# Attention windows as 64-row, 32- and 64-column products instead of zero-padded 128-row ones

## The chip, the core and the metric

The kernel runs on one core of a Trainium2 chip. The metric is the device time of one launch in microseconds. TensorE (PE in the profile) multiplies; VectorE (DVE), ScalarE (ACT) and GpSimd (POOL) do the elementwise work; SyncE (SP) issues nearly all DMAs. A matmul has a stationary operand, loaded into the array first (a weight load, PEld in the profile), and a moving operand that streams through; its result goes to one of eight PSUM banks of 128 partitions x 512 floats.

## What is computed

The reference, cut to what matters: attention in chunks of 32 queries over a window of 64 keys (8 memory keys, 16 to the left, the 32 of the chunk, 8 to the right), and then two feed-forward layers on 3072 tokens of 512 features.

```python
for c in range(nc):                       # 24 chunks of 32, for 4 batches and 8 heads of 64
    k_full = concat(mem_k, k[max(0, 32*c - 16) : min(S, 32*c + 40)])
    scores = matmul(q_c, k_full.T) / sqrt(D)
    a = softmax(scores)
    out[c] = matmul(a, v_full)
x = relu(out @ w_in)**2 @ w_out           # 512 -> 2048 -> 512
y = (silu(x @ w_gate) * (x @ w_val)) @ moe2_w_out   # 512 -> 1536 -> 512
```

Attention is in plain float32 on TensorE, where every matmul runs as two passes, each with its own weight load. The two layers split each operand into a high and a low part of the type float32r and sum three products.

## The kernel before

**Units.** Attention is cut into 24 units: 128 tokens (4 chunks) of one batch, all 8 heads. The host lays out, for each unit, `q`, `k` and `v` as 128 x 1024 floats. A partition of `q` and `k` is (one of two heads `hh`, one of 64 features); a partition of `v` is (one of two halves `m` of the heads, one of 64 keys of the window). Thus each 128-row operand holds two heads over each other.

**Scores** (`scores`, matmul at L544). For each of 16 (pair of heads, chunk) the stationary operand is 128 rows x 64 columns of `q`, the moving one 128 rows x 64 keys. So that the two heads stay apart, the host puts `q` down as a block diagonal: the 64 columns are 32 queries of the one head and 32 of the other, and half of the rows of each are zeros. The output stands in 64 PSUM partitions, alternately the lower and the upper half, so the array is used as two column halves of 128 rows x 64 columns.

**Weights** (`weigh`, L573 to L605). Maximum, subtract, Exp, sum, reciprocal, multiply, on a 128 x 512 tile `pt`, mostly on DVE.

**Turning.** The weights must stand with keys on partitions. Units 0 to 7 do that on TensorE (`turn_pe`, L644), and two copies of 64 x 512 (L653 on DVE, L655 on ACT) bring the result into a block-diagonal tile `pbd` (named `a` in the profile); the others use 16 transposes of 32 x 128 on DVE (`turn`, L622), which write into `pbd` as well. POOL sets two such tiles to zero at the start (L511), and only their blocks are ever written.

**Weighted sums** (`mixing`, matmul at L673). 16 matmuls: stationary 128 rows x 64 columns of `v`, moving 128 rows x 64 columns of `pbd`, again in two column halves, all into one PSUM bank.

**Leaving** (`leave`, L467 on ACT and L474 on DVE). The bank goes as a high and a low part, in one instruction of 512 columns on each engine, to the input tile `x` of the first layer. The last eight units go to DRAM by way of a copy (`leave_far`).

**The layers.** For four blocks of 512 tokens the first layer runs in the direct way: per hidden row block 12 matmuls of 512 columns into a hidden bank (L852), its ReLU, square and split on ACT, DVE and POOL, and 12 matmuls into four accumulating banks (L879), which lags two row blocks behind. In the first block the weights are decoded as they come (`prep1`, L731 to L819, which ends in the low part at L815). Then follow, from about 431 us, the rest of the first and all of the second layer with seven products in place of eight (L1108, L1245).

**What sets the order.** The code records operations with the engines that may do them and an estimated cost (`Plan.op`); a planner (`Plan.run`) then lays all of them out in one order for all engines, gives out the buffers, and keeps PE as busy as its costs say. `todo` says beside which hidden row block each step of a unit stands. From the second unit of the list `TURNS` on, the weighted sums of one unit and the scores of the next are one PE operation, with a planned cost of 2.2 us (L550), so that they stand directly behind each other; this is so 15 times. Buffers: twelve tiles `S0` for the `q`, `k`, `v` of the first four units, four tiles `A4` for the two `pbd` and the inputs of the rest, eight PSUM banks, of which the layer holds four for its accumulators.

The names in the rows: `ps` is a PSUM bank, `s` and `a` are tiles of `S0` and `A4`, `xx` and `x` the layer's inputs, `rp0` and so on decoded weights, `t` and `f` scratch tiles, `m` small statistics, `r` the split hidden values.

## Time and profile before

| what | value |
|---|---|
| time, median of 3 runs | 1105.41 us (1105.08 to 1106.93) |
| the profiled execution's own time | 1106.09 us |
| its span, first to last instruction | 1104.3 us |
| mean granted TensorE clock | 0.996 |
| PE busy | 1082.3 us, 98% of the span |
| PE weight loads busy | 892.0 us, 81% |
| DVE busy | 860.0 us, 78% |
| ACT busy | 594.1 us, 54% |
| DMA | 309.42 MB, mean 280 GB/s |

The shares are means over the whole program. A stage's own limit is read from the busy time by stretch, from the chain of work that ended last, and from who waits for whom. A group "x32" of L544 or L673 is 16 matmuls of two passes. Ends of matmuls are modelled in the profile, starts are not; lengths of groups are therefore best taken from start to start.

### The profile page before, as it was taken

The numbers are of one execution on the slowest core, as the hardware profiler recorded it, in microseconds if no ns is written. First come the engines' busy times: TensorE is split into PE (matmuls) and PEld (weight loads), VectorE is DVE, ScalarE is ACT, GpSimd is POOL, SyncE is SP. The second block draws the span as 40 slices with busy tenths as digits, with TensorE's granted clock in tenths as the row PEclk, the third lists the DMA queues.
The fourth block names the chain that finished last, engine by engine and source line by source line (L and its number), as shares of the span: only waits on it lengthen the run. The fifth ranks groups of instructions, "written<-read, shape, count | busy, mean of one in ns | idle before, by whom it ended". The sixth has DMA issues, their size and how long they took to land.

```text
span 1104.3 us, 17051 instructions
## 1 busy us (share of the span) xinstructions
PE 1082.3 (98%) x6044; PEld 892.0 (81%) x6044; DVE 860.0 (78%) x1540; ACT 594.1 (54%) x1010; POOL 126.5 (11%) x106
## 2 busy tenths in 40 slices
PE   5899999999999999999999999999999999999998
PEld 4778888888888888888888888888888887888886
DVE  6999878878879999778997667998769854534981
ACT  4888554554556566556654344564566633333650
POOL 2113101112011222001300000102310000000000
PEclk9899999999999999999999999999999999999999
DMA  9953487888889889999868999996998578655552
GB/s 362 409 222 113 134 278 242 296 294 300 306 277 344 288 285 342 393 344 348 290 225 266 404 406 395 328 357 224 358 335 298 161 241 307 213 195 172 190 169 99
DMA packets 133669, 309.42 MB, mean 280 GB/s; under 512 B 13136, under 2 KB 50000, under 8 KB 133584
## 3 DMA queue, kind: packets, MB, share of 16 engines
q1 hardware_dynamic: 133584, 308.33, 78.9%
q8 instruction: 48, 0.79, 0.3%
q14 instruction: 37, 0.30, 0.1%
HBM read 227.02 MB, written 81.26 MB: 279 GB/s over the span
## 4 chain that ended last, share of the span: by engine, by line
PE 95%; DMA 2%; ACT 1%; DVE 1%; issue 0%; SPq 0%; ACTq 0%
PE ps L1108 37%; PE ps L1245 22%; PE ps L852 16%; PE ps L879 15%; PE ps L673 2%; PE ps L544 2%; DMA rp0float<-in_w 1%; DMA s<-in_q 1%; ACT f L765 0%; SPq L525 0%; DVE u L486 0%; PE ps L644 0%; ACT f L772 0%; DVE f L486 0%; DVE rp3float32r L815 0%
## 5 line engine op out<-in xcount | busy, mean ns | idle before, releaser
L495 ACT ACTIVATE t<-ps 128x512 f32<-128x512 f32 x170 | 100.9, 596 | 218.4 <-PE ps L852 102.3
L486 DVE TENSOR_TENSOR t<-t,ps 128x512 f32<-128x512 f32 x72 | 49.1, 686 | 42.0 <-PE ps L1108 38.1
L622 DVE STREAM_TRANSPOSE a<-t 32x128 f32<-32x128 f32 x256 | 77.4, 303 | 4.3
L495 ACT ACTIVATE t<-t 128x512 f32<-128x512 f32 x72 | 45.3, 632 | 57.8 <-DVE t L486 57.4
L486 DVE TENSOR_TENSOR u<-u,u 128x512 f32<-128x512 f32 x70 | 48.2, 711 | 0.1
L474 POOL TENSOR_TENSOR r<-t,r 128x512 fp32r<-128x512 f32 x21 | 29.8, 1420 | 147.8 <-ACT r L467 107.8
L467 ACT ACTIVATE f<-f 128x512 fp32r<-128x512 f32 (+1 forms) x60 | 32.4, 546 | 15.3 <-DVE f L486 10.2
L474 DVE TENSOR_TENSOR f<-f,f 128x512 fp32r<-128x512 f32 (+1 forms) x52 | 32.7, 631 | 9.6 <-ACT f L467 9.2
L474 DVE TENSOR_TENSOR r<-t,r 128x512 fp32r<-128x512 f32 x32 | 22.1, 689 | 22.6 <-ACT r L467 22.5
L486 DVE TENSOR_TENSOR u<-ps,t 128x512 f32<-128x512 f32 x26 | 17.9, 689 | 26.5 <-PE ps L1108 24.9
L495 ACT ACTIVATE u<-ps 128x512 f32<-128x512 f32 x45 | 26.7, 595 | 20.6 <-PE ps L1108 20.3
L866 ACT ACTIVATE t<-t 128x512 f32<-128x512 f32 x56 | 35.3, 630 | 1.3
L467 ACT ACTIVATE r<-t 128x512 fp32r<-128x512 f32 x53 | 33.3, 629 | 1.5 <-DVE t L869 0.2
L486 DVE TENSOR_TENSOR u<-ps,u 128x512 f32<-128x512 f32 x34 | 23.4, 689 | 9.4 <-PE ps L1108 8.8
L585 ACT ACTIVATE t<-t 128x512 f32<-128x512 f32 x24 | 15.1, 630 | 22.3 <-DVE t L578 22.3
L673 PEld LDWEIGHTS ps<-a,a 128*64 128x64 f32 x640 | 20.3, 138 | 6.7 <-issue 4.9
L673 PE MATMUL ps<-a,a 128*64 128x64 f32 x640 | 23.0, 225 | 0.0
L544 PE MATMUL ps<-a,a 128*64 128x64 f32 x640 | 22.3, 223 | 0.0
L802 DVE CUSTOM_DVE_ANT_0 f<-f,f 128x2048 uint16<-128x2048 uint16 (+1 forms) x17 | 22.0, 1294 | 0.3
L544 PEld LDWEIGHTS ps<-a,a 128*64 128x64 f32 x640 | 20.4, 138 | 1.8 <-issue 1.4
L474 POOL TENSOR_TENSOR rp9float32r<-u,rp9float32r 128x512 fp32r<-128x512 f32 x2 | 5.9, 2972 | 127.2 <-ACT rp9float32r L467 115.9
L467 ACT ACTIVATE x<-u 128x512 fp32r<-128x512 f32 x26 | 16.3, 626 | 7.6 <-PE ps L1245 4.2
(836 smaller groups left out, 3096.9 us busy)
## 6 DMA issues: line engine op xcount, KB each, us to landing
tma<-f SPq DMA_DIRECT2D x31, 512.0 KB, 5.8
f<-in_w SPq DMA_DIRECT2D x21, 512.0 KB, 5.5
a<-in_q SPq DMA_DIRECT2D x20, 512.0 KB, 5.6
a<-in_k SPq DMA_DIRECT2D x20, 512.0 KB, 6.7
a<-in_v SPq DMA_DIRECT2D x20, 512.0 KB, 4.3
rp0float32r<-tma SPq DMA_DIRECT2D x14, 512.0 KB, 6.2
rp3float32r<-tma SPq DMA_DIRECT2D x12, 512.0 KB, 5.9
rp2float32r<-tma SPq DMA_DIRECT2D x11, 512.0 KB, 6.6
```

Of the source, the lines that this page charges most:

```text
L467: lambda: nc.scalar.activation(out=dst(HI), in_=src(), func=AF.Copy),
L474: eng.tensor_tensor(out=dst(LO), in0=src(), in1=dst(HI).bitcast(F32), op=ALU.subtract)
L486: eng.tensor_tensor(out=out[1](), in0=x[1](), in1=y[1](), op=op)
L495: nc.scalar.activation(out=out[1](), in_=x[1](), func=func)
L544: nc.tensor.matmul(o[64 * par : 64 * par + 64, s, f, m, :], q[:, s, m, ci, :], k[:, s, m, ci, :], start=True, stop=True,)
L622: nc.vector.transpose(out=o[g : g + 32, hh, :, :, m, :].rearrange("k s (f c) q -> k s f c q", c=2)[:, :, :, par, :], in_=a[r : r + 32, :, ...
L673: nc.tensor.matmul(o[64 * hh : 64 * hh + 64, 2 * s : 2 * s + 2, CH * ci : CH * ci + CH], a[:, hh, s, ci, :], b[:, hh, s, ci].rearrange("p ...
L852: nc.tensor.matmul(at(hp), w1of("in", i, a)[:, k * P : k * P + P], x[:, b, k, :], start=(n == 0), stop=(n == len(terms) - 1),)
L866: nc.scalar.activation(out=at(h), in_=at(h), func=AF.Square)
L879: nc.tensor.matmul(at(accs[m]), w1of("out", i, a)[:, m * P : m * P + P], at(h2)[:, 512 * b : 512 * b + 512], start=(i == 0 and n == 0), st ...
L1108: nc.tensor.matmul(at(bank), at(w[slot])[:, o : o + P], at(r[i, n])[:, 512 * b : 512 * b + 512], start=(first and n == 0 and m == 0), stop ...
L1245: nc.tensor.matmul(at(bank[i][n]), at(w[i][g // 2])[:, o : o + P], at(r)[:, 512 * b : 512 * b + 512], start=(first and m == 0), stop=(g == ...
```

## The change

The zeros go. `q` comes from the host as 128 x 512 floats, without the block diagonal, and takes up half of its tile. Each score matmul becomes two of half the size: stationary 64 rows x 32 columns, moving 64 rows x 64 columns, with row offset 0 or 64 by the head and column offset 0, 32, 64 or 96, so that four neighbours in the order stand in four different corners of the array. The weighted sums become 32 matmuls of 64 rows x 64 columns with 32 moving columns, in the four quarters of the array; since two quarters above each other write the same partitions, they go to two PSUM banks, one for each half `m` of the heads. The weights in turned form go to the free half of the unit's `q` tile; there is no `pbd` and no setting to zero. The turning by TensorE needs one copy of 128 x 512 in place of two of 64 x 512. Leaving is two steps of 256 columns on each engine in place of one of 512.

```diff
             for b, src in srcs:
                 pl.op(
-                    {"SP": 0.4}, lambda b=b, src=src: nc.sync.dma_start(out=at(b), in_=src[u]),
-                    (), (b,), move=rate(524288),
+                    {"SP": 0.4}, lambda b=b, src=src: nc.sync.dma_start(out=at(b)[:, : src.shape[-1]], in_=src[u]),
+                    (), ((b, 0),), move=rate(262144 if src is qd else 524288),
                 )
...
-                for p in range(4):
-                    s, m = p // 2, p % 2
-                    for ci in range(4):
-                        f, par = ci // 2, ci % 2
-                        nc.tensor.matmul(
-                            o[64 * par : 64 * par + 64, s, f, m, :], q[:, s, m, ci, :],
-                            k[:, s, m, ci, :], start=True, stop=True,
-                        )
+                for n in range(32):
+                    (s, m), f, par, hh = divmod(n // 8, 2), n // 4 % 2, n // 2 % 2, n % 2
+                    r, g = 64 * hh, 64 * par + 32 * hh
+                    nc.tensor.matmul(
+                        o[g : g + 32, s, f, m, :], q[r : r + 64, s, m, 2 * f + par, :],
+                        k[r : r + 64, s, m, 2 * f + par, :], start=True, stop=True,
+                        tile_position=(r, g),
+                    )
...
-            for m in range(2):
-                pl.op(
-                    {"ACT": 0.6, "DVE": 0.69} if self.start else {"ACT": 0.6},
-                    lambda e, m=m: spread(e, m), (tp,), [(pbd, 4 * m + n) for n in range(4)]
-                )
+            copy(
+                ((self.q, 1), lambda: at(self.q)[:, 512:]), whole(tp),
+                engs={"ACT": 0.6, "DVE": 0.69} if self.start else {"ACT": 0.6},
+            )
...
-                for s in range(2):
-                    for ci in range(4):
-                        for hh in range(2):
-                            nc.tensor.matmul(
-                                o[64 * hh : 64 * hh + 64, 2 * s : 2 * s + 2, CH * ci : CH * ci + CH],
-                                a[:, hh, s, ci, :], b[:, hh, s, ci].rearrange("p m q -> p (m q)"),
-                                start=True, stop=True,
-                            )
+                for n in range(32):
+                    s, ci, hh, m = n // 16, n // 4 % 4, n // 2 % 2, n % 2
+                    r, g = 64 * m, 64 * hh
+                    nc.tensor.matmul(
+                        at(x[m])[g : g + 64, P * s + CH * ci : P * s + CH * ci + CH],
+                        a[r : r + 64, hh, s, ci, :], b[r : r + 64, s, ci, hh, :],
+                        start=True, stop=True, tile_position=(r, g),
+                    )
...
         def leave(self, xb, a):
-            x = self.x
-            split(
-                lambda h: at(xb).rearrange("p (h k t) -> p h k t", h=2, k=KC)[
-                    :, h, :, a * P : a * P + P
-                ],
-                lambda: at(x).rearrange("p (k t) -> p k t", k=4), (x,), ((xb, a),),
-                diff=FROM,
-            )
+            for m, x in enumerate(self.x):
+                split(
+                    lambda h, m=m: at(xb).rearrange("p (h s m t) -> p h s m t", h=2, s=2, m=2)[
+                        :, h, :, m, a * P : a * P + P
+                    ],
+                    lambda x=x: at(x)[:, : 2 * P].rearrange("p (s t) -> p s t", s=2),
+                    (x,), ((xb, (a, m)),), n=256, diff=FROM2,
+                )
...
-    new_pbd()
-    new_pbd()
...
-        "q": qz.reshape(NU, P, 1024),
+        "q": qq.reshape(NU, P, 512),
```

`leave_far` is cut in two in the same way. The planned PE costs, 1.16 us for one group and 2.2 us for two joined ones, are not changed. Since buffers and costs differ, the planner gives another order; the kernel's line numbers fall by some 20 (scores stand at L532, weighted sums at L649, the hidden rows at L833, the second half of the layer at L860, the low part of decoded weights at L796).

PE, at one of the 15 places where the weighted sums of one unit (L673) and the scores of the next (L544) stand together, before:

```order
L852 MATMUL ps_91<-x_66,w14float32r 128x512 x12
L673 MATMUL ps_90<-a_67,a_70 64x2x32 x16
L544 MATMUL ps_93<-a_69,a_68 64x64 x16
L879 MATMUL ps_94<-r_65,w14float32r 128x512 x3
```

and such a place of the change:

```order
L860 MATMUL ps_92<-r_64,w15float32r 128x512 x3
L649 MATMUL ps_94<-a_67,a_69 64x32
L649 MATMUL ps_95<-a_67,a_69 64x32
...
L532 MATMUL ps_93<-a_68,a_70 32x64 x32
L833 MATMUL ps_89<-xx,rp0float32r 128x512 x12
```

The weighted sums take turns between two banks, 16 times each, and the two groups hold three banks where they held two.

ACT in the first 30 us, around the first decode of the weights `rp0` (L765, in the change L746), before:

```order
L655 ACTIVATE a_68<-ps_89 64x16x32
L467 ACTIVATE xx<-ps_90 128x4x128
L765 ACTIVATE f_75<-rp0float_217 128x1024
L772 ACTIVATE f_76<-rp0float_217 128x1024
L467 ACTIVATE xx<-ps_91 128x4x128
L765 ACTIVATE f_71<-rp1float_220 128x1024
```

and in the change:

```order
L468 ACTIVATE xx<-ps_90 128x2x128
L746 ACTIVATE f_75<-rp0float_215 128x1024
L468 ACTIVATE xx<-ps_91 128x2x128
L468 ACTIVATE xx<-ps_92 128x2x128
L468 ACTIVATE xx<-ps_93 128x2x128
L468 ACTIVATE xx<-ps_94 128x2x128
L468 ACTIVATE xx<-ps_95 128x2x128
L791 ACTIVATE rp8float32r<-f_72 128x512
L753 ACTIVATE f_76<-rp0float_215 128x1024
```

Before, one leaving step stands behind two decode steps of `rp0`; in the change five short ones stand behind one.

DVE in the first block of tokens, from the low part of `rp4` to that of `rp5`, before:

```order
L815 TENSOR_TENSOR rp4float32r<-f_73,rp4float32r 128x2x512
L802 ISA f_72<-f_72,f_74 128x2048
L474 TENSOR_TENSOR r_65<-t_77,r_65 128x512
L779 TENSOR_SCALAR f_75<-f_75 128x1024
L779 TENSOR_SCALAR f_71<-f_71 128x1024
L815 TENSOR_TENSOR rp5float32r<-f_72,rp5float32r 128x2x512
```

and in the change, where a unit's weighing (L562, L567, L578, L588, L592) stands between the two:

```order
L796 TENSOR_TENSOR rp4float32r<-f_73,rp4float32r 128x2x512
L562 TENSOR_REDUCE m_87<-ps_91 128x8
L760 TENSOR_SCALAR f_72<-f_72 128x1024
L567 TENSOR_TENSOR t_77<-ps_91,m_87 128x512
L767 TENSOR_SCALAR f_72<-f_72 128x1024
L760 TENSOR_SCALAR f_75<-f_75 128x1024
L775 SCALAR_TENSOR_TENSOR f_72<-rp5float_271,f_72 128x1024
L578 TENSOR_REDUCE m_86<-t_77 128x8
L783 ISA f_72<-f_72,f_74 128x2048
L588 RECIPROCAL m_86<-m_86 128x8
L767 TENSOR_SCALAR f_75<-f_75 128x1024
L592 TENSOR_TENSOR t_77<-t_77,m_86 128x512
```

Two rows on, behind one more step of `rp6`, the low part of `rp5` follows. The weighing of this unit stood behind `rp6` and `rp7` before.

## Rows read from the trace of the kernel before

**Rows 1.** The chain of work that ended last, shares of the span by line.
```profile
PE ps L1108 37%; PE ps L1245 22%; PE ps L852 16%; PE ps L879 15%; PE ps L673 2%; PE ps L544 2%; DMA rp0float<-in_w 1%; DMA s<-in_q 1%; ACT f L765 0%; SPq L525 0%; DVE u L486 0%; PE ps L644 0%; ACT f L772 0%; DVE f L486 0%; DVE rp3float32r L815 0%
```

**Rows 2.** By stretch: length, then busy PE, PEld, DVE, ACT, POOL; clock, DMA, GB/s.
```profile
30.00:66.00 36.00, 34.46 (x166) 27.18 (x167) 34.50 (x41) 31.58 (x42) 3.70 (x3) 0.93 1.02 405
66.00:110.00 44.00, 44.00 (x358) 35.75 (x357) 42.37 (x54) 37.86 (x52) 11.98 (x9) 1.00 0.34 114
110.00:431.00 321.00, 321.00 (x2311) 265.55 (x2310) 275.17 (x604) 176.52 (x307) 55.99 (x50) 1.00 0.80 280
431.00:1104.00 673.00, 668.67 (x2942) 551.31 (x2940) 488.46 (x809) 333.89 (x592) 48.55 (x32) 1.00 0.80 281
```

**Rows 3.** One joined pair of groups in order of time, PE: start, length, what.
```profile
288.62 2.88 PE L879 MATMUL ps<-r,rp7float32r 128*128 128x512 f32 x12
291.44 1.15 PE L673 MATMUL ps<-a,a 128*64 128x64 f32 x32
292.42 1.10 PE L544 MATMUL ps<-a,a 128*64 128x64 f32 x32
293.45 3.02 PE L852 MATMUL ps<-xx,rp8float32r 128*128 128x512 f32 x12
296.30 2.88 PE L879 MATMUL ps<-r,rp8float32r 128*128 128x512 f32 x12
299.02 0.62 PE L852 MATMUL ps<-xx,w10float32r 128*128 128x512 f32 x2
```

**Rows 4.** Score passes begun by 292.43, by 292.49 and by 292.55 us.
```profile
292.42 0.23 PE L544 MATMUL ps<-a,a 128*64 128x64 f32 x2
292.42 0.29 PE L544 MATMUL ps<-a,a 128*64 128x64 f32 x4
292.42 0.34 PE L544 MATMUL ps<-a,a 128*64 128x64 f32 x6
```

**Rows 5.** By line: durations in ns (least/median/most), first and last start.
```profile
L673 PEld LDWEIGHTS ps<-a,a x32: 132/138/138, 291.4 to 292.3; 128*64 128x64 f32 x32
L673 PE MATMUL ps<-a,a x32: 222/222/270, 291.4 to 292.4; 128*64 128x64 f32 x32
L852 PE MATMUL ps<-xx,rp8float32r x12: 389/389/497, 293.4 to 296.1; 128*128 128x512 f32 x12
L544 PE MATMUL ps<-a,a x640: 222/222/270, 37.9 to 388.8; 128*64 128x64 f32 x160
```

**Rows 6.** Start of the first layer, in order of time, ACT and PE.
```profile
27.07 1.12 ACT L765 ACTIVATE f<-rp0float 128x1024 f32<-128x1024 f32 x1 [1.58 <-DMA rp0float<-in_w]
29.12 0.58 ACT L467 ACTIVATE xx<-ps 128x512 fp32r<-128x512 f32 x1
29.75 8.19 PE L852 MATMUL ps<-xx,rp9float32r 128*128 128x512 f32 x24 [2.82 <-ACT xx L467]
```

**Rows 7.** One unit's weighing (first and last of five) and the low parts, DVE and PE.
```profile
40.29 0.68 DVE L573 TENSOR_REDUCE m<-ps 128x8 f32<-128x512 f32 x1
49.09 0.68 DVE L603 TENSOR_TENSOR t<-t,m 128x512 f32<-128x512 f32 x1
62.30 1.23 DVE L815 TENSOR_TENSOR rp4float32r<-f,rp4float32r 128x1024 fp32r<-128x1024 f32 x1
66.39 1.22 DVE L815 TENSOR_TENSOR rp5float32r<-f,rp5float32r 128x1024 fp32r<-128x1024 f32 x1
69.18 2.88 PE L852 MATMUL ps<-xx,rp5float32r 128*128 128x512 f32 x12
```

**Rows 8.** Groups by shape: count, busy us, mean ns, then idle before; half- and whole-width steps.
```profile
L486 DVE TENSOR_TENSOR f<-f 128x256 f32<-128x256 f32 x37 | 16.5, 447 | 0.3
L467 ACT ACTIVATE f<-f 128x256 fp32r<-128x256 f32 x22 | 9.0, 410 | 3.7 <-DVE f L486 3.7
L467 ACT ACTIVATE x<-ps 128x512 fp32r<-128x512 f32 x8 | 4.8, 595 | 2.3 <-PE ps L673 2.2
L474 DVE TENSOR_TENSOR xx<-ps,xx 128x512 fp32r<-128x512 f32 x8 | 5.5, 685 | 0.1
```

More of the change, by code (lines that the diff above doesn't have):

```diff
@@ L314 @@
 FROM = {"DVE": 0.69}
+FROM2 = {"DVE": 0.43}
 def rate(nbytes):
@@ L477, in split @@
             costs, low, list(reads) + [(b, (q, HI)) for b, q in keys], [(b, (q, LO)) for b, q in keys],
-            shared=diff is not FROM,
+            shared=diff not in (FROM, FROM2),
         )
@@ L503, in half @@
         return ((b, n), lambda: at(b)[:, n * w : n * w + w])
-    pbds = []
-    def new_pbd():
-        b = pl.buf("A4", "pbd")
-        pl.op(
-            {"POOL": 1.0}, lambda: nc.gpsimd.memset(at(b), 0.0), (), [(b, n) for n in range(8)]
-        )
-        pbds.append(b)
-    def pbd_of(b):
-        return at(b).rearrange("p (h s c m q) -> p h s c m q", h=2, s=2, c=4, m=2)
     class Unit:
@@ L622, in run @@
                         nc.vector.transpose(
-                            out=o[g : g + 32, hh, :, :, m, :].rearrange(
-                                "k s (f c) q -> k s f c q", c=2
-                            )[:, :, :, par, :],
-                            in_=a[r : r + 32, :, :, m, e, :],
+                            out=o[g : g + 32, :, :, par, hh, :], in_=a[r : r + 32, :, :, m, e, :]
                         )
@@ L646, in turn_pe @@
             pl.op({"PE": 0.64}, run, (pt,), (tp,), tail=0.2)
-            def spread(e, m):
-                o = 64 * m
-                dst = pbd_of(pbd)[o : o + 64, :, :, :, m, :].rearrange("k h s c q -> k h (s c) q")
-                src = at(tp)[o : o + 64].rearrange("k (g h q) -> k h g q", g=8, h=2)
-                if e == "DVE":
-                    nc.vector.tensor_copy(dst, src)
-                else:
-                    nc.scalar.activation(out=dst, in_=src, func=AF.Copy)
-            for m in range(2):
-                pl.op(
-                    {"ACT": 0.6, "DVE": 0.69} if self.start else {"ACT": 0.6},
-                    lambda e, m=m: spread(e, m), (tp,), [(pbd, 4 * m + n) for n in range(4)]
-                )
+            copy(
+                ((self.q, 1), lambda: at(self.q)[:, 512:]), whole(tp),
+                engs={"ACT": 0.6, "DVE": 0.69} if self.start else {"ACT": 0.6},
+            )
         def mixing(self):
-            v, pbd, x = self.v, self.pbd, pl.buf("PS", "x")
+            v, x = self.v, [pl.buf("PS", "x") for _ in range(2)]
             self.x = x
@@ L668, in run @@
                 a = at(v).rearrange("p (h s c d) -> p h s c d", h=2, s=2, c=4)
-                b, o = pbd_of(pbd), at(x).rearrange("p (k t) -> p k t", k=4)
-                for s in range(2):
-                    for ci in range(4):
-                        for hh in range(2):
-                            nc.tensor.matmul(
-                                o[64 * hh : 64 * hh + 64, 2 * s : 2 * s + 2, CH * ci : CH * ci + CH],
-                                a[:, hh, s, ci, :], b[:, hh, s, ci].rearrange("p m q -> p (m q)"),
-                                start=True, stop=True,
-                            )
-            return run, (v, pbd), (x,)
+                b = at(self.q)[:, 512:].rearrange("p (s c h q) -> p s c h q", s=2, c=4, h=2)
+                for n in range(32):
[6 more added lines that the diff above has]
+                    )
+            return run, ((v, 0), *((self.q, n) for n in self.q.parts if n)), x
         def mix(self):
@@ L685, in leave @@
         def leave(self, xb, a):
-            x = self.x
-            split(
-                lambda h: at(xb).rearrange("p (h k t) -> p h k t", h=2, k=KC)[
-                    :, h, :, a * P : a * P + P
-                ],
-                lambda: at(x).rearrange("p (k t) -> p k t", k=4), (x,), ((xb, a),),
-                diff=FROM,
-            )
+            for m, x in enumerate(self.x):
[6 more added lines that the diff above has]
+                )
         def leave_far(self, n, a):
             t = pl.buf("T2", "xt")
-            copy(whole(t), whole(self.x), engs={"ACT": 0.6, "DVE": 0.69})
+            for m, x in enumerate(self.x):
+                copy(
+                    ((t, m), lambda m=m: at(t).rearrange("p (s m t) -> p s m t", s=2, m=2)[:, :, m, :]),
+                    (x, lambda x=x: at(x)[:, : 2 * P].rearrange("p (s t) -> p s t", s=2)),
+                    engs={"ACT": 0.41, "DVE": 0.43},
+                )
             c = n * NT + a * P
@@ L1487, in _layout @@
     q8 = q.reshape(B, 2, 2, 2, UPB, 4, CH, D)
-    qz = np.zeros((B, UPB, 2, D, 2, 2, 4, 2, CH), f)
-    for hh in range(2):
-        qz[:, :, hh, :, :, :, :, hh, :] = q8[:, :, :, hh].transpose(0, 3, 6, 1, 2, 4, 5)
+    qq = q8.transpose(0, 4, 3, 7, 1, 2, 5, 6)
     k8 = kw.reshape(B, 2, 2, 2, UPB, 4, WIN, D)
```

16 lines of the change are left out of this document (8 added, 8 removed).

## The prediction

> **What bounds the kernel now.** I read the chain of work that ended last first: it lies on PE nearly throughout, and the lines that the change touches, scores (L544) and weighted sums (L673), hold 2% each [rows 1]. Then the busy time by stretch: from 66 to 431 us PE is busy without a gap, and later it misses 4.3 of 673 us [rows 2]. So from 66 us on every microsecond added to or taken from a PE group appears in the time, and work taken from DVE, ACT, POOL or the DMAs does not. From 30 to 66 us PE still works 34.46 of 36 us, but DVE 34.50: both are nearly full, and a gain on one engine is worth what the other lets through. Before 30 us nothing is computed by the layers; that stage ends when the first L852 starts, at 29.75 us [rows 6].
>
> Next the price of one group. In order of time, a joined pair (weighted sums, then scores) starts at 291.44, the scores begin at 292.42, the layer goes on at 293.45 [rows 3]. An undisturbed twelve-matmul group takes 2.72 us (296.30 to 299.02). The group before should thus have ended at 291.34, and the one behind, whose successor starts at 296.30, should have begun at 293.58: the pair costs 2.24 us. Inside it, passes begin two at a time: two of the scores' passes have begun 0.01 us after the group's start, four by 0.07, six by 0.13 [rows 4]; that is a beat of 0.058 us, and 16 beats are 0.93 us (0.98 between the two group starts, less the 0.05 below). Two passes that begin within 10 ns on 64 columns each are two column halves at work side by side. The rest of the 2.24, 0.38 us, is getting in (0.10 before the first start, 0.05 for the first weights) and out (0.23).
>
> What sets the beat? Two things could: the 64 moving columns, or the load of the 64 stationary ones. The first pass of a group has to wait for its weights, and it is 48 ns longer than the others (270 against 222); behind the scores the first pass with 128 stationary columns is 108 ns longer than the rest (497 against 389) [rows 5]. So a load of 64 columns takes about 50 ns, of 32 about 27 (an estimate by proportion). The moving side I get by elimination: 512 columns in one pass of the layer take 2.72/12 = 227 ns, but of another number type, so that row is only a floor of 28 ns for 64 columns; 58 ns is the ceiling. The load alone thus explains nearly the whole beat.
>
> **The change, part by part.** *Weighted sums.* 32 matmuls, 64 passes, in four corners: 16 beats of four. The moving columns fall from 64 to 32, but the stationary ones stay at 64, and their load of 50 ns still has to come once per pass in every corner. If all four corners run side by side, the beat is bounded below by that load, 0.05, and I see no reason for less than the 0.058 of today; with each more pass of a beat costing something, bounded by the 10 ns within which two start now, it is up to 0.063. *Scores.* The stationary columns halve, the moving ones stay at 64: again one of the two legs remains, and again 16 beats of four. So the number of beats does not fall in either group, nor does the longer leg: 0 to +5 ns per beat, 0 to +0.08 us per group. There are 640/32 = 20 groups of scores [rows 5] and as many of weighted sums behind the start stage: 0 to +3.2 us in all. I take the middle, +1.6.
>
> *Shape of the corners.* Today both groups of a pair use 128 x 64 corners, and nothing is lost between them. Now the sums use 64 x 64 and the scores 64 x 32. No row shows a step between two small shapes. It may be free, as today between the groups, or cost what getting out costs, 0.23 us. I take the getting in, 0.15, since the next weights must again be loaded unhidden: 15 pairs x 0.15 = +2.25 us (0 to 3.5).
>
> *Start.* Four `q` of 512 KB become 256 KB ahead of all weights: 1.05 MB at the 405 GB/s of a full queue [rows 2] let `rp0` land 2.6 us earlier. Today the first L852 waits 2.82 us for a leaving step on ACT, which stands behind a decode that waits for `rp0` [rows 6]. So up to -2.6 us. But DVE must first have weighed and left all four units, and has two leaving steps of some 0.45 us per unit in place of one of 0.69 [rows 8]. What follows takes some back: one unit's weighing, five steps of 0.68, 0.68, 0.67, 0.20 and 0.68 = 2.9 us (the first and the last of them in [rows 7]), now stands between the low parts of `rp4` and `rp5`. Today `rp5` is ready at 67.6 and PE comes to it at 69.18, a cover of 1.6 us [rows 7]; 1.3 of the 2.9 remain as a wait, and more where the order puts further steps of `rp6` there. Net -2.6 to +1; I take -0.5.
>
> *What costs nothing.* Leaving in two halves adds 2 x 0.41 - 0.60 = 0.2 us per unit on ACT and 2 x 0.45 - 0.69 = 0.2 on DVE [rows 8]; behind 66 us both stand beside a PE that waits for neither, DVE with 46 of 321 us idle and ACT with 144 [rows 2]. If that cover were gone, the 16 later units would cost 3 us. The third bank of a joined pair leaves one for the hidden rows beside four accumulators; its eviction has the 2.72 us of the next L879 group to end in. Setting to zero on POOL and the bytes of the later `q` are off the path. The single copy in turning saves ACT 0.6 us for each of eight units, where ACT does not hold PE.
>
> *Sum.* +1.6 + 2.25 - 0.5 = +3.35 us on the profiled execution's 1106.09, which is 0.7 above the median: 1108.8, say **1109 us**. By the ends of the terms (0 to 3.2, 0 to 3.5, -2.6 to +1) this case runs from 1103 to 1113. About 0.2%, 2.2 us, is what a measurement of this kernel can tell from no change.
>
> **The rivals.** *The sums get faster.* If the beat follows the moving columns, because the load hides deeper than I think, a beat of the sums is half of 0.058, 0.029: 16 x 0.029 less on each of 20 groups, -9.3 us, and with the other terms (half of the 1.6 for the scores, 2.25, -0.5) -6.7: 1099. For it: both legs lie near the beat, so rows cannot exclude it. Against it: the 48 ns that a first pass waits. It decides as soon as the sums' group is under 0.8 us.
>
> *Upper and lower corners take turns.* Rows show only column halves side by side, none above each other. If the two rows of quarters in the sums cannot run together, they need 32 beats, +0.93 us on 20 groups = +18.6: with the forecast's terms 1127. Scores have each corner in its own column strip and would be spared.
>
> *One bank for two rows of corners.* In the scores, corners of upper and lower rows write one bank, in different partitions. The price from rows is the same, 32 beats in place of 16, +18.6 us, 1127. The Trainium skill, TensorEngine Tiling (Array Packing), Gotcha 1: PSUM Pressure, says that different row tiles cannot access the same PSUM bank at once; no row here shows row tiles, and by that rule the scores would pay, while by the rows' column halves they would not.
>
> *Passes come no faster.* Today one pass begins per 0.029 us on the mean. If that is the pace at which PE takes load and matmul, 64 passes need 1.86 us in either group: +0.93 on 40 groups, 37 us, 1145. Against it: pairs begin within 10 ns, so instructions wait for the array, not the array for them [rows 4]. The Trainium skill, TensorE: Matmul & The Clock Gate, section "Wait — 56ns, not 53.3ns?", has start-to-start never below about 25 ns, however few the columns; as a mean that would be an estimated 1.6 us per group and 1135; the two starts within 10 ns speak against it as a floor between neighbours, and cannot as a mean.
>
> *The start keeps its 2.6 us* and the steps between shapes are free: 1103 to 1106.
>
> **How the numbers follow.** Forecast 0.55 (of it 0.03 faster, 0.18 same, 0.34 slower); faster sums 0.09; corners taking turns in the sums 0.16; one bank 0.05; the pace of passes 0.10; the start kept 0.05 (0.04 same, 0.01 faster). Faster 0.13, same 0.22, slower 0.65. The range from 1103 to 1128 leaves out the faster sums, a little of the start, and the pace of passes. The forecast's own range is 1103 to 1113.
>
> **What would show it.** In the profile after, scores and sums have 64 passes per group. Their starts in one joined pair settle most: sums to scores about 0.98 to 1.1 us, scores to the next layer group about 1.03 to 1.1, plus 0.15 between. A distance of 0.5 from sums to scores is the faster rival; 1.9 there alone, the rows of quarters taking turns; 1.9 in the scores alone, the bank; both, the pace. Four passes begun within 0.03 us would show four corners side by side. The first layer group should start at 27 to 29.5 us, with a wait for `rp5` near 65 us. I am wrong at the root if PE has waits of a microsecond behind 110 us: then banks, not passes, decide.

## The result and the profile after

The changed kernel takes **1120.53 us** (median, 1119.46 to 1121.18), the kernel before 1105.46 beside it: 1.0133 times as long, 95% interval 1.0115 to 1.015. The profiled execution after is 1120.37 us long, its span 1118.7 (before 1104.3). The sign was forecast, the size was not: the sum had +3.35 us, the chip +15.1, and no rival describes where they came in.

To find the place, I number the 4476 matmuls of 512 columns (the layers' own) of either trace by their start, and compare start n with start n. The first two rows are read so; the others belong to the experiments below.

```
matmul n                     0     36    100    300   1500   2100   2900   4475
start before, us         29.75  41.80  58.70 113.53 423.05 559.05 740.38 1099.90
changed kernel, later by +1.21  +1.47  +4.90  +3.77  +5.70 +10.16 +14.68  +14.64
e1 (corners, old order)  +1.83  +1.14  +1.15  +0.97  +2.43  +2.44  +2.44   +2.32
e2 (late corners only)   -1.04  -1.34  -1.35  -1.52  -0.04  -0.04  -0.04   +0.03
e6 (start: wide sums)    -2.02  -2.95  -2.93  -3.06  -1.60  -1.59  -1.59   -1.04
e4 (late wide, new order)+1.22  +0.88  +4.40  +3.43  +3.99  +7.90 +12.42  +13.04
e5 (late POOL on DVE)    +1.37  +1.55  +5.00  +3.91  +5.91  +5.91  +5.91   +7.10
e13 (wide, new order, e5)+0.87  +0.58  +4.13  +4.66  +5.34  +5.34  +5.34   +5.42
```

Between n = 36 and n = 100 the new order has one group of scores (1.03 us) that the old order has later, at 71.99 us; by n = 300 both have done the same groups. So there are four losses: 1.5 us up to 42 us, 2.3 more up to 114, 1.9 in the rest of the stage of groups up to 423, and 8.9 behind it, in two steps. The first is uncertain by about 2 us: e2 and e12 begin with the same program as the kernel before, and stand at -1.3 and -2.3 by n = 36. First the groups, on which the prediction spent most words. One joined pair after, PE in order of time, answers to [rows 3]:

```profile
150.47 1.14 PE L649 MATMUL ps<-a,a 64*64 64x32 f32 x64
151.53 1.10 PE L532 MATMUL ps<-a,a 64*32 64x64 f32 x64
152.56 3.03 PE L833 MATMUL ps<-x,rp1float32r 128*128 128x512 f32 x12
```

Sums (now L649) to scores (L532) is 1.06 us for 0.98, scores to the next layer group 1.03 as before. Twice the passes in the same time: four corners work side by side.

The two steps behind 431 us, as waits of PE in that stretch (total, times, longest):

```profile
PE ps L1089 <- DVE u L487: 2.5, 1, 2.5
PE ps L1089 <- DVE a L487: 1.8, 1, 1.8
PE ps L1226 <- DMA x<-tmb: 0.3, 1, 0.3
```

The busy times by stretch show what is new there (columns as in [rows 2]). First come three rows of after, then two of before that [rows 2] did not split:

```profile
30.00:66.00 36.00, 31.30 (x260) 24.83 (x257) 33.50 (x39) 31.02 (x41) 8.50 (x5) 0.93 0.95 377
431.00:560.00 129.00, 127.19 (x554) 104.63 (x553) 106.76 (x170) 74.28 (x131) 27.48 (x19) 0.99 0.90 329
560.00:740.00 180.00, 177.19 (x773) 145.75 (x772) 148.15 (x248) 90.17 (x166) 26.15 (x15) 0.99 0.94 345
```

```profile
431.00:560.00 129.00, 129.00 (x571) 106.82 (x570) 110.54 (x190) 76.66 (x137) 12.82 (x9) 1.00 0.95 342
560.00:740.00 180.00, 180.00 (x796) 149.05 (x795) 143.47 (x251) 91.30 (x165) 9.42 (x6) 1.00 0.94 339
```

The fifth busy time is POOL's: 27.48 us in 19 steps for 12.82 in 9, and 26.15 in 15 for 9.42 in 6. DVE has 20 steps fewer in the first stretch and is hardly less busy (106.76 for 110.54). The change touches nothing there. But the planner orders all engines at once, from 135 us on steps of the later stages stand between the attention's, and other lengths of the attention's steps make it choose another order and give other steps to POOL. What that does, ahead of the wait of 2.5 us, DVE, POOL and PE in order of time:

```profile
720.49 1.78 DVE L1030 TENSOR_TENSOR f<-f,f 128x512 f32<-128x512 f32 x1
722.20 1.78 DVE L475 TENSOR_TENSOR rp1float32r<-u,rp1float32r 128x512 fp32r<-128x512 f32 x1
723.90 1.77 DVE L1030 TENSOR_TENSOR f<-f,ff 128x512 f32<-128x512 f32 x1
725.59 1.51 DVE L487 TENSOR_TENSOR ff<-f 128x256 f32<-128x256 f32 x1
```

```profile
720.10 1.63 POOL L475 TENSOR_TENSOR x<-u,x 128x512 fp32r<-128x512 f32 x1 [3.22 <-ACT x L468]
721.69 1.74 POOL L475 TENSOR_TENSOR rp0float32r<-u,rp0float32r 128x512 fp32r<-128x512 f32 x1
723.39 1.73 POOL L475 TENSOR_TENSOR rp7float32r<-a,rp7float32r 128x512 fp32r<-128x512 f32 x1
725.09 1.74 POOL L487 TENSOR_TENSOR u<-a,u 128x512 f32<-128x512 f32 x1
```

```profile
727.12 1.52 PE L1226 MATMUL ps<-rp1float32r,rp6float32r 128*128 128x512 f32 x6
731.10 1.30 PE L1089 MATMUL ps<-rp0float32r,rp3float32r 128*128 128x512 f32 x3 [2.47 <-DVE u L487]
```

Four DVE steps that alone take 0.68, 0.68, 0.68 and 0.41 us take 1.78, 1.78, 1.77 and 1.51, each beside a POOL step: 4.4 us more. PE then stands 2.47 us and comes out of it at half the clock (three matmuls in 1.30 for 0.84). From 731.10 to 735.55 us, at a mean granted clock of 0.62, twelve matmuls take 4.45 us in place of 2.72: the wait and these 1.7 us are nearly the whole step.

The other step begins at 548.6 us. Ahead of it DVE is stretched in the same way: from 541.09 to 547.4 us four steps that alone take 0.42, 0.42, 0.68 and 0.68 us take 1.51, 1.52, 1.78 and 1.77, while POOL is at work from 540.85 to 548.58. The DVE step on `a` (L487) comes late by it, and PE waits 1.81 us. Twelve matmuls then take 4.44 us in place of 2.72, at a mean granted clock of 0.61. Behind the wait DVE is stretched once more (550.60 to 556.66, with POOL at work from 550.42 to 556.37), and SP's queue, which issues in order, adds the wait of 0.3 us. DVE, then SP:

```profile
541.09 2.95 DVE L440 TENSOR_SCALAR f<-f 128x512 int32<-128x512 int32 x2
543.96 3.48 DVE L448 SCALAR_TENSOR_TENSOR f<-gg,f 128x512 int32<-128x512 int32 x2
550.60 1.77 DVE L475 TENSOR_TENSOR f<-f,f 128x512 fp32r<-128x512 f32 x1
555.14 1.52 DVE L487 TENSOR_TENSOR f<-ff,f 128x256 f32<-128x256 f32 x1
```

```profile
545.58 0.58 SPq L1001 DMA_DIRECT2D rp7float32r<-tmb  x1
552.39 3.18 SPq L977 DMA_DIRECT2D tmb<-f  x3
558.20 0.42 SPq L1001 DMA_DIRECT2D x<-tmb  x1
```

The stores of a prepared weight (L977) wait for the steps from 550.60 on, and the load of `x` that PE needs at 565.00 stands behind them.

In the start, PE's own order of time shows two stops inside a group, with no step that is waited for:

```profile
13.30 0.64 PE L532 MATMUL ps<-s,s 64*32 64x64 f32 x29 [0.75 <-DMA s<-in_k]
15.74 0.75 PE L532 MATMUL ps<-s,s 64*32 64x64 f32 x35 [1.81 <-issue]
23.81 2.80 PE L649 MATMUL ps<-s,s 64*64 64x32 f32 x139
28.79 1.71 PE L649 MATMUL ps<-s,s 64*64 64x32 f32 x53 [2.18 <-issue]
30.96 7.71 PE L833 MATMUL ps<-xx,rp8float32r 128*128 128x512 f32 x24 [0.47 <-ACT xx L468]
```

and then, from 42 to 63 us, DVE's decoding is late for `rp1` and `rp3`, with POOL steps beside it once more (DVE, POOL, PE):

```profile
40.26 2.33 DVE L775 SCALAR_TENSOR_TENSOR f<-rp1float,f 128x1024 int32<-128x1024 int32 x1
44.24 1.79 DVE L767 TENSOR_SCALAR f<-f 128x1024 int32<-128x1024 int32 x1
54.89 2.32 DVE L775 SCALAR_TENSOR_TENSOR f<-rp3float,f 128x1024 int32<-128x1024 int32 x1
58.87 1.21 DVE L775 SCALAR_TENSOR_TENSOR f<-rp4float,f 128x1024 int32<-128x1024 int32 x1
```

```profile
39.68 1.82 POOL L475 TENSOR_TENSOR r<-t,r 128x512 fp32r<-128x512 f32 x1 [18.98 <-ACT r L468]
43.34 2.13 POOL L475 TENSOR_TENSOR r<-t,r 128x512 fp32r<-128x512 f32 x1 [1.84 <-ACT r L468]
54.60 1.52 POOL L475 TENSOR_TENSOR r<-t,r 128x512 fp32r<-128x512 f32 x1 [3.36 <-ACT r L468]
```

```profile
47.82 3.02 PE L833 MATMUL ps<-xx,rp1float32r 128*128 128x512 f32 x12 [1.66 <-DVE rp1float32r L796]
53.92 1.10 PE L532 MATMUL ps<-a,a 64*32 64x64 f32 x64
62.57 3.02 PE L833 MATMUL ps<-xx,rp3float32r 128*128 128x512 f32 x12 [1.88 <-DVE rp3float32r L796]
```

POOL's busy time from 30 to 66 us is 8.50 us where it was 3.70 [rows 2]; L775 takes 2.33 and 2.32 us beside it, and 1.21 without. Before, PE waits 1.00 us for `rp2` and 0.37 for `rp3` in this stretch:

```profile
57.66 3.02 PE L852 MATMUL ps<-xx,rp3float32r 128*128 128x512 f32 x12 [0.37 <-DVE rp3float32r L815]
```

### The profile page after: what moved, and what is told of

It is laid out like the page before. It is cut to its first block, busy times and chain, and to the rows that moved or that the text cites. A ratio compares the mean times of both kernels' runs of the same rounds, so it can differ in the third digit from the quotient of the medians.

```text
span 1118.7 us, 20168 instructions
## 1 busy us (share of the span) xinstructions
PE 1089.8 (97%) x7580; PEld 896.2 (80%) x7580; DVE 867.2 (78%) x1556; ACT 589.1 (53%) x1022; POOL 142.3 (13%) x108
## 4 chain that ended last, share of the span: by engine, by line
PE 92%; DVE 2%; DMA 2%; issue 1%; ACT 1%; SPq 0%; ACTq 0%
PE ps L1089 36%; PE ps L1226 21%; PE ps L833 16%; PE ps L860 15%; PE ps L649 2%; PE ps L532 2%; DMA s<-in_k 1%; DMA x<-tmb 1%; DVE f L487 1%; DMA f<-win 0%; DMA f<-in_w 0%; PE ps L631 0%; DVE u L487 0%; DVE ff L487 0%; ACT t L496 0%
## 5 line engine op out<-in xcount | busy, mean ns | idle before, releaser
L496 ACT ACTIVATE t<-ps 128x512 f32<-128x512 f32 (+1 forms) x171 | 99.6, 584 | 234.7 <-PE ps L833 108.0
L487 DVE TENSOR_TENSOR t<-t,ps 128x512 f32<-128x512 f32 x72 | 48.7, 683 | 41.5 <-PE ps L1089 39.6
L475 POOL TENSOR_TENSOR r<-t,r 128x512 fp32r<-128x512 f32 x26 | 39.4, 1514 | 210.4 <-ACT r L468 166.4
L487 DVE TENSOR_TENSOR u<-u,u 128x512 f32<-128x512 f32 x68 | 44.9, 681 | 0.1
L487 POOL TENSOR_TENSOR u<-u,u 128x512 f32<-128x512 f32 x9 | 17.3, 1930 | 189.9 <-DVE u L487 116.6
L487 DVE TENSOR_TENSOR u<-ps,u 128x512 f32<-128x512 f32 x34 | 23.4, 688 | 12.9 <-PE ps L1089 12.5
L487 DVE TENSOR_TENSOR u<-ps,t 128x512 f32<-128x512 f32 x24 | 16.5, 689 | 19.7 <-PE ps L1089 19.6
L475 DVE TENSOR_TENSOR r<-t,r 128x512 fp32r<-128x512 f32 x27 | 18.8, 698 | 15.8 <-ACT r L468 13.0
L574 ACT ACTIVATE t<-t 128x512 f32<-128x512 f32 x24 | 15.1, 628 | 25.4 <-DVE t L567 25.4
L649 PEld LDWEIGHTS ps<-a,a 64*64 64x64 f32 x1280 | 20.5, 135 | 7.0 <-issue 4.6
L468 ACT ACTIVATE f<-ff 128x256 fp32r<-128x256 f32 (+1 forms) x29 | 14.9, 517 | 16.0 <-DVE ff L487 14.3
L649 PE MATMUL ps<-a,a 64*64 64x32 f32 x1280 | 22.7, 220 | 0.0
L532 PE MATMUL ps<-a,a 64*32 64x64 f32 x1280 | 22.0, 218 | 0.0
L562 DVE TENSOR_REDUCE m<-ps 128x8 f32<-128x512 f32 x24 | 16.4, 682 | 6.4 <-PE ps L532 6.3
```

The lines of the kernel that those rows point to most:

```text
L468: lambda: nc.scalar.activation(out=dst(HI), in_=src(), func=AF.Copy),
L475: eng.tensor_tensor(out=dst(LO), in0=src(), in1=dst(HI).bitcast(F32), op=ALU.subtract)
L487: eng.tensor_tensor(out=out[1](), in0=x[1](), in1=y[1](), op=op)
L496: nc.scalar.activation(out=out[1](), in_=x[1](), func=func)
L532: nc.tensor.matmul(o[g : g + 32, s, f, m, :], q[r : r + 64, s, m, 2 * f + par, :], k[r : r + 64, s, m, 2 * f + par, :], start=True, stop=True,
L649: nc.tensor.matmul(at(x[m])[g : g + 64, P * s + CH * ci : P * s + CH * ci + CH], a[r : r + 64, hh, s, ci, :], b[r : r + 64, s, ci, hh, :], ...
```

## The experiments

**Order or matmuls?** Theory A: the 8.9 us behind 431 come from the order alone, the groups cost some 0.04 us a pair. Rival B: the corners or the second bank hold PE up. To part them, e1 puts the changed matmuls under the order of before: the planner sees before's steps, lengths and buffers, and gives the same order on every engine; only what a step issues is exchanged. The second PSUM bank of the sums is one that this order leaves free; for two of the 24 units there is none, and they keep full-height sums.

```diff
+CS = set(range(24))
+CX = set(range(24))
...
+                if self.u in CS:
+                    return self.corner_scores(sc)
...
+        room = [n for n in taken if all(b < lo or a > hi for a, b in taken[n])]
...
+        if x.u in CX and room:
+            second[x] = room[0]
```

> The changed matmuls in the order of the kernel before: every engine's order, every buffer and the steps on POOL are those of before; scores of all units, and sums of the 22 units for which that order leaves a second PSUM bank free, run in four corners, with half-size q loads (two units keep their sums at full height). Theory A (most of the 15 us came in behind 431 us, by another order in which POOL takes more steps and slows DVE; the groups themselves cost 0.04 us a pair): the 9.0 us lost behind 431 us are gone, the start's loss (4.9 us by 63 us, with two stops of PE of 1.8 and 2.2 us for which no wait shows) stays in part: 1107 to 1111. Rival B (the corners or the second bank hold PE up wherever they stand, by buffers that come free late): as the changed kernel, 1118 to 1121. Rival C (all of it is the order, the start too): 1105 to 1107.

e2 takes the four start units out (`CS`, `CX` from 4 on).

```diff
-CS = set(range(24))
-CX = set(range(24))
+CS = set(range(4, 24))
+CX = set(range(4, 24))
```

> As e1_corners_old_order, but the four units of the start stage keep the full-height matmuls and the full-size q; only the 20 later units run in corners. Theory A: the start is that of the kernel before; what is left is about 20 groups of sums by 0.05 us each, +1.0, so 1106 to 1107, and the difference to e1 is what the corners cost in the start, 2 to 5 us. Rival B: 1116 or more. If the start's loss comes from order alone, e1 and e2 are alike within 1 us.

e4 is the other way round, the changed kernel's order with full-height matmuls behind the start:

```diff
+OLD = set(range(4, 24))
...
+                if self.u in OLD:
+                    return self.wide_scores(sc)
```

> The changed kernel's order, buffers and engines, with the 20 later units back to full-height matmuls (zeros again beside the queries and beside the weights, which stand in the place of the unit's own q); the four units of the start stay in corners. Theory A: start and the losses behind 431 us remain, only the groups give back their 1.0 us: 1119 to 1120. Rival B (corners or their bank are the cause): 1106 to 1111.

And e5 tests the mechanism on the changed kernel itself:

```diff
+    late = len(pl.ops)
...
     for o in order:
+        if o.eng == "POOL" and o.n >= late:
+            o.eng = "DVE"
```

> The changed kernel, with one edit: the 55 steps of the second layer's stages and of its weights that the order gives to POOL run on DVE, at the same places of the order. Theory A with its mechanism (DVE's 0.68 us steps take up to 1.78 us while POOL works, and two chains on DVE then hold PE up for 4.5 and 4.4 us, at 544 to 565 and 728 to 731 us): both stalls shrink to under 1.5 us each, 1111 to 1114. Rival D (the order on SP's queue, stores ahead of the loads that PE needs, is the cause, not POOL): the stalls stay, 1119 to 1121. Rival E (37 us more on DVE make it the bound): over 1121.

Measured: e1 1109.39 us (1.0041 of before, 1.0026 to 1.0056), e2 1105.42 (1.0004, 0.9995 to 1.0014), e4 1118.98 (1.0129, 1.0114 to 1.0144), e5 1111.19 (1.0059, 1.0044 to 1.0074). All four fall where theory A put them (e2 0.6 below its range). With the old order the corners lose nothing behind 431 us; with the new order the loss stays though the late corners are gone. The groups themselves have a price of their own: from n = 300 to 1500 the corners lose 1.5 us in the old order (e1, e2), full height in the new order 0.6 and 0.7 (e4, e13), both together 1.9 and 2.0 (changed kernel, e5). The time of e2 does not show it; its interval reaches from 0.6 us below before to 1.5 above. In e5 both stalls are gone; PE there, at the same two groups as at 727.12 and 731.10 above, and the stretch by engine:

```profile
722.72 1.52 PE L1226 MATMUL ps<-rp1float32r,rp6float32r 128*128 128x512 f32 x6
724.08 0.84 PE L1089 MATMUL ps<-rp0float32r,rp3float32r 128*128 128x512 f32 x3
```

```profile
431.00:560.00 129.00, 129.00 (x571) 106.82 (x570) 106.82 (x196) 77.46 (x138) 0.00 (x0) 1.00 0.94 339
560.00:740.00 180.00, 180.00 (x796) 149.05 (x795) 146.69 (x265) 92.23 (x170) 0.00 (x0) 1.00 0.94 346
```

DVE takes 196 steps in place of 170 and is as busy as in the changed kernel, 106.82 us for 106.76. Rival D, SP's order as the first cause, falls with it: that order is unchanged in e5. A wait of 1.6 us for an ACT step at 932 us is new in e5 and was not looked into.

**What costs in the start?** e1 and e2 differ by 4.0 us, all of it from the corners of four units and their smaller `q`. e6 gives the start its full-height sums back (`CX` from 4 on), e8 its full-height scores and full-size `q` (`CS` from 4 on).

> As e1_corners_old_order (1109.4 us: corners everywhere, order of before), but the four units of the start stage keep full-height sums; their scores stay in corners, with the half-size q. Theory F (in the start, bursts of 128 and more small passes outrun the supply of instructions: PE stops for about 2 us, without a wait that shows, beside a 16 KB packet of the instruction queue, and the clock is low behind it): with 128 passes fewer in the start at least one of the stops ahead of the first layer goes, and rp0 still lands earlier than before: 1104 to 1107. Rival G (the corners' scores alone hold the start up): as e1, 1108 to 1110. Rival H (the stops come from sums in two banks and from their two leaving steps): 1103 to 1105, with no stop left at all.

> As e1_corners_old_order, but the four units of the start stage keep full-height scores and the full-size q; their sums are in corners. Theory F: 128 passes fewer in the start, so at least one stop fewer than e1, but the first layer's weights land as late as before: 1105.5 to 1108, behind e6 by 0 to 2.6 us. Rival G (corners' scores hold the start up): 1105 to 1106. Rival H (sums in corners do): as e1, 1108 to 1110.

e7 leaves the corners out and doubles the passes:

```diff
-                for p in range(4):
+                for p in [n for n in range(4) for _ in range(2 if self.start else 1)]:
...
-                for s in range(2):
+                for s in [n for n in range(2) for _ in range(2 if self.start else 1)]:
```

> The kernel before, with the passes of the start stage's four scores groups and four sums groups issued twice (the same values written again): 64 full-height passes per group, as many instructions as with corners, no corner anywhere. Theory F (number of instructions): stops of PE of over 1.2 us appear ahead of the first layer where no step of another engine or load is waited for, beside an instruction packet, and the first layer starts 1 to 4 us later than 29.75; 1106 to 1110. Rival G (corners cause the stops): no such stop, groups of 2 us at the full clock, first layer within 1 us of 29.75; 1105 to 1106.5.

e10 keeps e1's corners, and takes the start's groups corner by corner:

```diff
+                if self.start:
+                    par, hh, s, m, f = n // 16, n // 8 % 2, n // 4 % 2, n // 2 % 2, n % 2
...
+                        if self.start:
+                            m, hh, s, ci = n // 16, n // 8 % 2, n // 4 % 2, n % 4
```

> As e1_corners_old_order (two stops of PE above 2 us ahead of the first layer, each beside a packet of the instruction queue), with the corner groups of the four start units issued corner by corner: same instructions, same corners, banks and steps behind them, but about 0.05 us per pass in place of 0.016. Theory F2 (it is the pace: passes that begin every 16 ns use up 16 KB of instructions, some 128 passes, in about as long as the next packet takes to come): no stop without a named wait of over 1 us in or right ahead of a group, though the groups take 3.2 us each at the full clock. Rival G (the corners or the second bank stop PE): the stops stay at 1.8 us or more.

Measured: e6 1105.42 us (1.0003, 0.9994 to 1.0011), e8 1108.14 (1.0028, 1.0017 to 1.004), e7 1108.78 (1.0037, 1.0025 to 1.0049), e10 1136.19 (one run). So the start's price is that of its **sums** in corners; scores in corners and their smaller loads together cost nothing. The granted clock differs with the sums, e1 first, e6 second (15 to 22 and 22 to 31 us):

```profile
15.00:22.00 7.00, 4.82 (x136) 4.02 (x134) 4.67 (x11) 3.58 (x7) 2.55 (x4) 0.56 1.03 410
22.00:31.00 9.00, 5.97 (x200) 5.45 (x200) 6.72 (x16) 5.27 (x10) 0.00 (x0) 0.77 1.03 407
```

```profile
15.00:22.00 7.00, 5.04 (x140) 4.10 (x140) 5.93 (x13) 4.17 (x8) 2.55 (x4) 1.00 1.03 407
22.00:31.00 9.00, 5.72 (x79) 4.44 (x80) 8.81 (x14) 7.89 (x11) 0.00 (x0) 1.00 1.03 406
```

In e1 the clock lies for long at the lower level (1.2 of 2.4 GHz; the means are 0.56 and 0.77), after PE had waited 1.88 us for a POOL step; a group of sums takes 1.9 us there, for 1.1 at the full clock. In this execution the clock falls at 15.8 us, ahead of the first group of sums (16.85), where e1 and e6 still run the same program. But the mean granted clock of all executions goes with the sums: 0.989 to 0.993 in e1, 0.993 to 0.995 in e8, 0.996 to 1.000 in e6. Why, and how much of the 4.0 us is clock, is not shown.

My theory F on e1 failed, however. The stop of 2.28 us that I had read as a want of instructions in e1 is also in e8, where the profile names the step that PE waits for. PE in e1, then in e8:

```profile
22.11 1.94 PE L714 MATMUL ps<-a,s 64*64 64x32 f32 x64 [2.28 <-issue]
```

```profile
21.77 1.14 PE L714 MATMUL ps<-a,s 64*64 64x32 f32 x64 [2.29 <-DVE xx L765]
```

It is an ordinary wait, for the leaving of the unit before: in e8 its two halves on DVE (L765) run from 20.92 to 21.68 us, behind the copy of the weights (20.21). Before, the wait at this place is for that copy alone, and 1.47 us long. e7 has as many passes in its groups and no stop of over 0.5 us in one: 64 full-height passes take 2.1 to 2.4 us there, and its 3.9 us are, by elimination, those passes themselves (its time lies where theory F put it, 1106 to 1110, but without theory F's stops). e10 tells nothing about stops inside groups, of which e1 had none to remove; the wait of 2.28 us is there again (2.29). Its passes took 0.08 to 0.09 us each where 0.05 was expected, since PE ran at the lower level through the whole start: the 512-column matmuls behind the groups begin 0.43 us apart up to 62.7 us, and 0.23 from there on. The first granted clock that this trace holds is of 62.7 us, so the 1.00 that a stretch ahead of it shows is not a reading.

The two stops inside groups are real in the changed kernel's order alone: after the same 221 passes of scores and 139 of sums in the changed kernel, e4 and e5. e13, all full-height in that order (`OLD` for all units, and e5's edit), asks what they cost.

> The changed kernel's order, buffers and banks, with no corner left: all 24 units with full-height scores and sums (zero-laid q of full size, weights with zeros in its place, leaving in two halves as the order has it), and the late POOL steps on DVE as in e5_after_late_on_dve (1111.2 us, start 4.9 us behind the kernel before at 63 us). It asks what of the start's loss belongs to the corners' passes. Theory F2 (two stops of PE in the start, in the middle of groups after 221 passes of scores and 139 of sums, come from corner passes that use up their instructions faster than the next 16 KB arrive; half the instructions at half the pace do not): no stop inside a group, start's loss 0.5 to 3 us, 1106 to 1108.5. Rival I (the start's order alone, with weighing between the decodings, costs the 4.9 us): the loss by 63 us stays at 4 to 6 us, 1109 to 1111.

Measured: 1110.88 us (1.0044, 1.003 to 1.0057). The stops are gone, and the loss is not. PE in e13, the start's last three groups of sums and the two late layer groups:

```profile
25.45 3.20 PE L696 MATMUL ps<-s,s 128*64 128x64 f32 x96
46.94 3.01 PE L895 MATMUL ps<-xx,rp1float32r 128*128 128x512 f32 x12 [1.67 <-DVE rp1float32r L858]
61.73 4.60 PE L895 MATMUL ps<-xx,rp3float32r 128*128 128x512 f32 x12 [1.87 <-DVE rp3float32r L858]
```

The waits for `rp1` and `rp3` are those of the changed kernel to 0.01 us. From n = 36 to 100 the new order comes later by 3.4, 3.5, 3.5 and 3.6 us (changed, e4, e5, e13), of which 1.0 is the group of scores that it has there and the old order has not; the old order loses nothing (e1, e2, e6): rival I holds. In e13 the wait for `rp3` costs another 1.6 us by the clock (twelve matmuls in 4.60 us for 3.02), which is why it stands at +4.66 by n = 300. That POOL's share makes the greater part of the loss is read from the rows above and not tried. Nor is the price of the two stops: e13 lacks them, but also loads the large `q`.

**The halves of the change, and the beat.** e11 is scores in corners with small `q` loads and no more (`CX` empty), e12 late sums in corners and no more (`CS` empty, `CX` from 4 on), both in the old order.

> The scores' half of the change alone, in the order of before: scores of all 24 units in corners, with half-size q loads; sums, weights with zeros, their bank and their steps as before. Theory A: the groups of scores cost nothing (1.03 us in both kernels), the start gains what e6_start_wide_sums showed in its trace (1.0 to 2.9 us by the first layers), nothing is lost behind it: 1102 to 1104. If half-size loads are worth nothing, or the corners of the scores cost the start as much as they bring: 1104.5 to 1106.

> The sums' half of the change alone, in the order of before, for the units behind the start: 18 of 20 groups of sums in corners; scores, q loads and the start as before. Theory A: 18 groups by 0.07 us (1.06 in place of 0.98 or 0.99): +1.2 to +1.5, 1105.9 to 1106.9, and behind e11 by 2 to 4 us. If sums in corners cost nothing: 1104.5 to 1105.5.

Measured: 1106.02 us (1.0003, 0.9994 to 1.0012) and 1106.09 (1.0003, 0.9994 to 1.0012), beside a before of 1106.07. Neither half helps or hurts by more than such times can tell. In e11 theory A failed: the gain of 2 to 4 us did not come. The smaller loads' gain in the start, 1.9 us in e11's trace at n = 36, lies within what equal starts differ by from one execution to the next (e2 and e12, with no corner in the start, show -1.3 and -2.3 there), and the groups give part of it back. No version came out ahead of the kernel before.

e9 is e2 with the sums issued corner by corner:

```diff
-                        s, ci, hh, m = n // 16, n // 4 % 4, n // 2 % 2, n % 2
+                        m, hh, s, ci = n // 16, n // 8 % 2, n // 4 % 2, n % 4
```

> As e2_late_corners_old_order (1105.4 us), with the passes of each corner group of sums issued corner by corner (8 matmuls, 16 passes, of one corner after the other) in place of going round the four corners. If the beat of 0.058 us holds per corner and PE overlaps only neighbours of its queue, a group takes up to 64 x 0.058 = 3.7 us in place of 1.06: 18 groups, up to +48 us, 1130 to 1153. If PE looks far enough ahead to fill the other corners, the group stays at 1.1 us: 1105 to 1107.

Measured: 1151.47 us (one run). One pair of it, PE:

```profile
302.98 3.29 PE L714 MATMUL ps<-a,a 64*64 64x32 f32 x64
306.20 1.10 PE L549 MATMUL ps<-a,a 64*32 64x64 f32 x64
```

306.20 - 302.98 = 3.22 us for 64 passes is 0.050 us per pass: just the weight load of 64 columns that [rows 5] gave. Here corners work side by side only where the program goes round them.

## Why the prediction was right in sign and wrong in size

- *What bounds the kernel.* Right as far as it went: PE, and the end follows it. But that "work taken from DVE, ACT, POOL or the DMAs does not" appear in the time was read from the old order, in which PE has no wait for DVE of over 0.3 us behind 66 us. The step that failed is the sum: it had no term for the order behind 431 us, and that term is 8.9 of 14.6 us: two waits of PE for DVE steps that POOL stretches, and the lower clock behind each. The place was to be seen beforehand, since the order of those engines moves with the change; I priced the instructions that it moves next to the attention, and not those later.
- *The range.* The forecast's own range, 1103 to 1113, was missed. That 1120.53 lies between 1103 and 1128 is luck: the upper end came from rivals at 1127, and neither of them took place.
- *Weighted sums, scores, shape of the corners.* The mechanism held, the sizes were too large. +1.6 for beats and +2.25 for steps were forecast; in the order of before, the small groups and transposes from 66 to 431 us take 42.1 us in all (e1, e2) for 40.9, +1.2. Time from sums to scores plus from scores to the layer: full height in both 0.98 + 1.03, corners in both 1.06 + 1.03, scores alone in corners (e11) 1.08 + 1.03, sums alone (e12) 1.06 + 1.08. A group of corners ahead of a layer group is 0.02 to 0.05 us *shorter* than today's 1.08; a step between shapes costs about 0.1, where the term took 0.15.
- *Start.* Forecast -0.5, measured +3.8 by 114 us. The two leaving steps and the weighing between decodings were named, with a cover of 1.6 us and an overhang of 1.3 at `rp5`. The waits came at `rp1` and `rp3`, 1.66 and 1.88 us, and none at `rp5`. By the rows POOL's steps slowed the decoding; this was not tried. On that reading, costing DVE's queue with the durations of before was the error.
- *What costs nothing.* Right for ACT, the bank and the DMA behind the start (e2); wrong for DVE's extra leaving in the start, where sums in corners cost some 4 us (e1 against e6): PE waits for the leaving, and the clock is lower; the shares were not parted.
- *Rivals.* Faster sums fell (1.06, not 0.5), and so did corners taking turns and one bank (1.06 and 1.03, not 1.9). The rule of the Trainium skill, TensorEngine Tiling (Array Packing), Gotcha 1: PSUM Pressure, would have cost the scores 0.9 us a group; no such time is in the rows. Passes that come no faster fell too: 64 in 1.03 us is 16 ns each on the mean. By the Trainium skill, TensorE: Matmul & The Clock Gate, section "Wait — 56ns, not 53.3ns?", it would be at least 25; the trace does not agree.
- *"I am wrong at the root if PE has waits of a microsecond behind 110 us: then banks, not passes, decide."* The waits came, the reason given for them did not: e1 and e5 have the second bank and neither of the two waits, e4 has the waits and no late corners.

## What to carry to other kernels

Where a planner orders all engines at once, a change in one stage is a new order for every stage: hold the old order and exchange only what the steps issue, and the change has its own price (here 1.5 us by the traces for the late corners, too little for the times to show), apart from that of the order. An engine with idle time is not free when its steps slow another's: look for steps at twice their length and for what runs beside them, and give the neighbour's work to the engine that waits. What small matmuls in corners cost is here set by the weight load per corner, and corners overlap only if the program goes round them: twice the passes took the same time, not less.

## What the runs showed of the hardware

- A DVE step whose operands all lie in SBUF can take 1.5 to 1.8 us in place of 0.41 or 0.68 beside POOL steps of 1.3 to 1.7; sixteen steps of the changed kernel that read PSUM and stand beside POOL keep their 0.67 to 0.69 (L487, 128x512). It can also be POOL that waits: in the changed kernel six such DVE steps in a row from 773.59 us take 0.68 each, and the POOL step beside them takes 5.31 (from 773.13). 26 more steps on DVE, and none on POOL, left DVE's busy time where it was (e5). The Trainium skill, SBUF — State Buffer, section "SBUF: two separate sides", says that the two share a pair of ports under an exclusive lock that the one that starts first holds for its whole instruction; the steps above agree.
- Corner passes begin every 16 ns on the mean where four corners take turns in the program, every 50 in a single one (e9). A step from one tile shape to another costs 0.08 to 0.13 us a pair.
- In the changed kernel's start PE stops for 2.0 and 2.4 us from one pass of a group to the next (1.81 and 2.18 without work), behind its first 449 and 962 recorded instructions, each beside one 16 KB packet of the instruction queue (13.25 to 14.32 and 26.39 to 27.50 us). A third packet, from 20.35 to 21.46 us, has no such stop beside it. That the packet is the reason is argued, not shown.
